# First six attention steps: bonus sums on TensorE, value copies on ScalarE, two weight pieces and the constants through ScalarE's queue

## The chip, the cores and the metric

One NeuronCore of one Trainium2 chip runs the whole program. The metric is the device time of one execution in microseconds (us). The engines are TensorE (PE in the rows, with its weight loads as PEld), VectorE (DVE), ScalarE (ACT), GpSimd (POOL) and SyncE (SP), which here only issues DMAs.

## The reference, cut to what matters

Three layers follow each other: a linear attention with a decaying state (4 batches, 8 heads, 768 tokens, 48 channels a head), a feed-forward layer with softplus (3072 tokens, 384 to 2048 to 384), and a layer of 8 experts with a greedy capacity-limited assignment.

```
for t in range(S):                                   # attention
    cur = einsum('bhd,bhe->bhde', u[None] * k_t, v_t)
    y[:, :, t] = einsum('bhd,bhde->bhe', r_t, state + cur)
    state = w[None, :, :, None] * state + einsum('bhd,bhe->bhde', k_t, v_t)
h = x @ w_in                                         # feed-forward
x = (maximum(h, 0) + log1p(exp(-abs(h)))) @ w_out
logits = x @ w_gate                                  # then the choice of an expert for each token,
out[mask] = maximum(x[mask] @ w1[e], 0) @ w2[e]      # and its two matmuls
```

The term `cur` is the bonus: for each token and head the sum over d of r·u·k, times the value row. Feed-forward weights arrive as 64-bit floats and are rebuilt to 32 bits with integer operations.

## The kernel before, in words

**Attention.** 24 steps of 128 rows each: step n takes 64 tokens of a pair of batches. `load_step` issues eight 96 KB DMAs for a step, all on SP's queue: k, r and v by token (tiles `kn`, `rn`, `vn`, line 367, two each) and v again in another layout (tile `X`, line 373, two). `attention(n)` then multiplies k and r by tables of powers (`ks`, `rs`, line 340), transposes both on PE (lines 466 and 470), copies them out of PSUM (`kT`, `ar`), multiplies (line 491), masks on DVE (`ar`, line 499), updates the state (lines 520, 525 and 527, copied into the next `X`) and forms the output (line 553). The bonus runs on DVE: `rk` = r·k, `rk`·`ut`, a reduction to `sd` (line 543), and `sv` = v·`sd`; line 558 adds `sv` to the output and makes `xf`. `xf` is transposed (line 566) into `xt`, the input of the feed-forward layer.

**Feed-forward.** 8 blocks of 384 tokens, three attention steps each. Block 0 runs in 32-bit floats, while the weights are being rebuilt: `from_double` loads a 384 KB piece into one of four buffers (tile `third`; line 607 for the first matrix, `w_in`, 16 pieces; line 624 for the second, `w_out`, 16 pieces) and rebuilds it with three DVE instructions (lines 599, 601 and 603). `ffn1(0, f)` (line 673) needs the transposed outputs of steps 0, 1 and 2 and piece f. Later blocks use split 16-bit weights (line 678). Blocks overlap: while block b runs its first matmul, block b-1 or b-2 runs its second, and the attention steps of a later block are woven in.

**What sets the order.** Every piece of work is an item with an engine (or a choice of two), an assumed duration, dependencies and a due time. `lay_out` plays the schedule through with the assumed durations, picks at each point the ready item with the earliest due time, and writes each engine's instruction stream in that order; on the chip every engine runs its stream in order and waits on semaphores. The due times come from `due_att`, `due_ffn1`, `due_ffn2` and a table of leads (`T0`, `ATT0`, `LOADL`, `AHEAD`, `HALFL`, `BITL`, `OUTLATE` and so on). `keep_warm` puts matmuls on a zero tile (`still`, line 143) into the gaps of the planned PE stream; their results are not used. All DMAs share eight completion semaphores in turn, so the ninth DMA waits at its issue for the first to land.

Of the kernel before, what the change touches and what calls it, by code (L numbers as in the profile page):

```python
# [21 lines left out]
def tile_kernel(ctx, tc, r, k, v, w, u, w_in, w_out, w_gate, w1, w2, out):  # L22
# [10 lines left out]
    HP = H // 2  # L33
# [114 lines left out]
    def lay_out(todo, rank, clock, warm=False):  # L148
# [91 lines left out]

    ACT.add_instruction(mybir.InstLoadActFuncSet(
        name=nc.get_next_instruction_name(), engine=mybir.EngineType.Activation, ins=[], outs=[],
        act_func_set_id=[a.name for a in SETS].index("natural_log_exp_and_others")))

# [5 lines left out]

    T0 = 15500.0
    LEN0 = 43500.0
# [20 lines left out]

    AHEAD = 7500.0

    TURNED, TURN = 6, 1500.0
    HALFL = 4000.0
    HALFL2 = -4000.0
    NLAT = 6
    LATL = 400.0  # L280
    OUTLATE = 5000.0
    RAWL = 17600.0
    BITL = 14000.0
    SPLITL = -3900.0
    WOUTL = 6100.0
    ATT0 = 2600.0
    LOADL = 1600.0

# [18 lines left out]
    XF = several(work, 2, [128, H * D], FT, "xf")  # L307
    XHL = several(work, 2, [128, 2 * DM], HF, "xhl")
    XT2 = several(ffn1p, 2, [128, 2 * KC, BT], HF, "xt")
# [50 lines left out]
    def load_step(n):  # L360
        GROUP[0] = "att"
        b0, s0 = step_tok(n)
        i = n % 2
        due = due_att(n) - LOADL
        for key, src, store in (("kn", k, KN), ("rn", r, RN), ("vn", v, VN)):
            for b in range(2):
                op("sp", 650.0, lambda b=b, src=src, store=store: SP.dma_start(
                    store[i][b * 64:(b + 1) * 64], src[b0 + b, :, s0:s0 + C, :].rearrange("h s d -> s h d")),
                    w=[(key, i, b)], due=due, size=546.0)
        for q in range(2):  # L370
            src = bass.AP(tensor=v.tensor, offset=v.offset + ((b0 * H + q) * S + s0) * D,
                          ap=[[D, C], [2 * S * D, 2 * HP], [1, D]])
            op("sp", 650.0, lambda q=q, src=src: SP.dma_start(
                X[n % 3][(1 - q) * 64:(2 - q) * 64, q].rearrange("p b a d -> p (b a) d"), src),
                w=[("xv", n % 3, q)], due=due + 3.0, size=546.0)

# [12 lines left out]
    DVE.memset(wt, 1.0)  # L389
    op("sp", 1300.0, lambda: [SP.dma_start(wt[q * 64:q * 64 + D], w.rearrange("(p q) d -> q d p", q=2)[q])  # L390
                              for q in range(2)], w=["wt"], due=-1e9, size=168.0)
    op("sp", 450.0, lambda: SP.dma_start(
        ut, bass.AP(tensor=u.tensor, offset=u.offset, ap=[[0, 128], [1, H * D]])), w=["ut"], due=-500.0, size=546.0)
    op("sp", 450.0, lambda: SP.dma_start(gate, w_gate.rearrange("(k p) e -> p k e", p=128)),
# [17 lines left out]
    def powers():  # L412
# [5 lines left out]
        for i in range(6):  # L418
# [3 lines left out]
            DVE.tensor_mul(pw[:, 1, :, C - 2 * m:C - m], pw[:, 1, :, C - m:C], f)  # L422

    op("dve", 3200.0, powers, r=["wt"], w=["pw", ("ar", 1, 0)], due=-1e8)

# [18 lines left out]
    def attention(n):  # L444
# [62 lines left out]
        if n % PC < PC - 1:  # L507
# [27 lines left out]
            for q in range(2):  # L535
                rows = slice(q * 64, (q + 1) * 64)
                op({"act": 413.0, "dve": 470.0}, 0.0, lambda eng, rows=rows, q=q: copied(eng, X[y][rows, q], wx[rows].rearrange("p a b d -> p b a d")),
                   r=[("wx", 0), ("wx", 1)], w=[("st", y, q)], due=due + 3)


        product(rk, RN[i], KN[i], rnk + knk, ["rk"], due + 3)
        product(rk, rk, ut.rearrange("p (h d) -> p h d", h=H), ["ut"], ["rk"], due + 3)
        op("dve", 470.0, lambda: DVE.tensor_reduce(sd, rk, axis=AX.X, op=OP.add), r=["rk"], w=[("sd", i)], due=due + 3)
        product(sv, VN[i], sd[:, :, None].to_broadcast([128, H, D]), vnk + [("sd", i)], [("sv", i)], due + 3)

# [35 lines left out]
        else:  # L581
            xh, xl = XHL[i][:, :DM], XHL[i][:, DM:]
            op(FROM_SBUF, 0.0, lambda eng: scaled(eng, xh, xf, 64.0), r=[("xf", i)], w=[("xhl", i, 0)], due=due + 5)
            op("dve", 470.0, lambda: DVE.scalar_tensor_tensor(xl, xf, 64.0, xh, op0=OP.mult, op1=OP.subtract),
# [8 lines left out]
    def from_double(src, t, key, due):  # L593
        c = WN[0]
        WN[0] += 1
        raw = RAW[c % 4]
        op("sp", 450.0, lambda: src(raw), w=[("raw", c % 4)], due=due - RAWL, size=1092.0)
        hi, lo = [raw[..., i] if len(t.shape) == 2 else raw[..., i].rearrange("p (k f) -> p k f", k=KC) for i in (1, 0)]
# [7 lines left out]
    def prep_win(j):  # L606
        from_double(lambda raw: SP.dma_start(
            raw.rearrange("p (k f) t -> p k (f t)", k=KC),
            w_in.rearrange("(k p) f -> p k f", p=128)[:, :, 256 * j:256 * (j + 1)]),
            WF32[j].bitcast(I32), ("wi", j + 1), due_ffn1(0, j))  # L610
# [10 lines left out]
    def prep_wout(f):  # L621
        due = due_ffn2(0, 0, f) - WOUTL
        t = WU32[f]
        from_double(lambda raw: SP.dma_start(
            raw.rearrange("p m t -> p (m t)"), w_out.rearrange("(c p) m -> c p m", p=128)[f]),
# [14 lines left out]
        op(FROM_PSUM, 0.0, lambda eng: copied(eng, wT, b1.view(KC, 128)), w=[wt], due=due, bank=b1)  # L640
        op("pe", 330.0, mm, r=[wt, "gate"], due=due, bank=b2)
        op("act", 58.0, lambda: ACT.copy(t[:, DM:], b2.view(E)), w=[("wg", f + 1)], due=due, bank=b2)
# [741 lines left out]
    for p in range(E):  # L1384
# [7 lines left out]
        experts(p)  # L1392
    total = lay_out(items, lambda it: (it.prio, it.n), {}, True)
    s_ps.close()
# [24 lines left out]
```

## Time and profile before

| | |
|---|---|
| median of 3 runs | 778.96 us (777.51 to 786.61) |
| the profiled execution, its own time | 775.64 us |
| its span, first to last instruction | 773.9 us |
| mean granted TensorE clock | 0.996 |
| busy: PE / weight loads / DVE / ACT / POOL | 749.8 / 493.0 / 624.9 / 404.1 / 81.2 us |

The span is what the trace covers; the execution's own time is 1.7 us longer. PE's busy time contains the zero matmuls of line 143 and is modelled at its ends, so its idle time is read together with the chain of waits.

### The profile page before, as it was taken

Reading aid. Unit: us, or ns where it says so; the run is one execution under the profiler, and the core shown is the slowest. Engines: PE = TensorE matmul, PEld = TensorE weight load, DVE = VectorE, ACT = ScalarE, POOL = GpSimd, SP = SyncE. Lnnn points to the kernel's source line nnn. Section 1 sums busy time; section 2 is a strip of 40 time slices with the busy share of each in tenths; the row PEclk is TensorE's granted clock in tenths of the full one; section 3 lists DMA queues with packets and bytes.
Section 4 is the critical chain, followed back from the end, with each engine's and each line's share of the span. In section 5 each row is a group of like instructions: output and inputs, shape, how many; then the busy total and the mean of one; then the engine's idle time right before and its main releaser. Section 6 shows DMA issues by size and latency. Waiting matters only on the chain.

```text
span 773.9 us, 18327 instructions
## 1 busy us (share of the span) xinstructions
PE 749.8 (97%) x7202; PEld 493.0 (64%) x7202; DVE 624.9 (81%) x1711; ACT 404.1 (52%) x808; POOL 81.2 (10%) x109
## 2 busy tenths in 40 slices
PE   7999999999999999999999999999999999998996
PEld 6865677666566666667676666666666665655663
DVE  7898998999998787788999977887789879877420
ACT  2165533799766666567889911211145424436731
POOL 1000000000000000000001000000232131317731
PEclk9999999999999999999999999999999999999999
DMA  7887764412343233333110003441385664837700
GB/s 137 172 183 191 211 171 77 83 22 62 69 91 66 56 68 62 62 67 71 36 22 11 2 12 94 118 121 50 97 208 165 174 175 143 211 108 191 216 31 30
DMA packets 170901, 80.04 MB, mean 103 GB/s; under 512 B 136512, under 2 KB 166464, under 8 KB 170816
## 3 DMA queue, kind: packets, MB, share of 16 engines
q1 hardware_dynamic: 167744, 69.44, 38.3%
q0 software_dynamic: 3072, 9.44, 4.0%
q8 instruction: 56, 0.92, 0.5%
q14 instruction: 29, 0.24, 0.1%
HBM read 61.55 MB, written 9.63 MB: 92 GB/s over the span
## 4 chain that ended last, share of the span: by engine, by line
PE 67%; DVE 18%; issue 4%; ACT 4%; DMA 4%; SPq 1%; POOL 1%; POOLq 0%; ACTq 0%; DVEq 0%
PE bank L678 14%; PE bank L1292 7%; PE bank L788 7%; PE bank L789 6%; PE bank L790 6%; PE bank L785 3%; PE bank L1310 3%; PE bank L1312 3%; PE bank L1311 3%; PE bank L553 2%; PE bank L673 2%; DVE ar L499 2%; DVE gf L691 2%; PE bank L1036 2%; DMA mraw<-moe_w 1%
## 5 line engine op out<-in xcount | busy, mean ns | idle before, releaser
L678 PEld LDWEIGHTS <-wi 128*128 128x128 f16 x1008 | 97.3, 98 | 65.2 <-issue 2.0
L678 PE MATMUL bank<-xt,wi 128*128 128x384 f16 x672 | 127.6, 326 | 0.0
L684 ACT ACTIVATE ta<-bank 128x384 f32<-128x384 f32 x128 | 61.5, 482 | 43.3 <-PE bank L678 30.2
L789 PE MATMUL bank<-wo,g 128*128 128x384 f16 (+1 forms) x240 | 78.4, 327 | 0.9 <-DVE wo L649 0.7
L788 PE MATMUL bank<-wo,g 128*128 128x384 f16 (+1 forms) x240 | 78.5, 327 | 0.0
L790 PE MATMUL bank<-wo,g 128*128 128x384 f16 (+1 forms) x240 | 78.5, 327 | 0.0
L691 DVE SCALAR_TENSOR_TENSOR gf<-bank,ta 128x384 f32<-128x384 f32 x112 | 61.8, 553 | 17.2 <-ACT ta L686 16.0
L678 PE MATMUL bank<-xs,wi 128*128 128x384 f16 x336 | 72.9, 326 | 0.0
L1292 PE MATMUL bank<-g,w1h 128*128 128x384 f16 x384 | 72.9, 326 | 0.0
L685 ACT ACTIVATE ta<-ta 128x384 f32<-128x384 f32 x128 | 66.5, 522 | 2.9
L686 ACT ACTIVATE ta<-ta 128x384 f32<-128x384 f32 x128 | 66.2, 519 | 2.5
L1312 PE MATMUL bank<-w2h,g 128*128 128x384 f16 x192 | 62.6, 326 | 0.0
L1310 PE MATMUL bank<-w2h,g 128*128 128x384 f16 x192 | 62.6, 326 | 0.0
L1311 PE MATMUL bank<-w2l,g 128*128 128x384 f16 x192 | 62.5, 326 | 0.0
L1296 ACT ACTIVATE g<-bank 128x384 f16<-128x384 f32 x64 | 30.7, 489 | 40.4 <-PE bank L1292 24.7
L1292 PEld LDWEIGHTS <-w1h 128*128 128x128 f16 x384 | 35.8, 98 | 22.6 <-issue 0.4
L1299 DVE SCALAR_TENSOR_TENSOR g<-bank,g 128x384 f16<-128x384 f32 x64 | 34.1, 548 | 19.4 <-ACT g L1296 19.3
L698 DVE SCALAR_TENSOR_TENSOR g<-gf,g 128x384 f16<-128x384 f32 x80 | 44.0, 553 | 3.1 <-ACT g L345 1.8
L499 DVE TENSOR_TENSOR ar<-bank,mask 64x256 f32<-64x256 f32 x96 | 40.5, 422 | 4.6 <-PE bank L491 2.3
L345 ACT ACTIVATE x2o<-bank 128x384 f16<-128x384 f32 x19 | 9.3, 490 | 65.3 <-PE bank L790 39.2
L1205 POOL DMA_INDIRECT third<-x2d,idx x24 | 25.8, 1074 | 155.7 <-DVE db L1009 130.0
L1292 PE MATMUL bank<-g,w1l 128*128 128x384 f16 x192 | 41.7, 326 | 0.0
(227 smaller groups left out, 1533.3 us busy)
## 6 DMA issues: line engine op xcount, KB each, us to landing
mraw<-moe_w SPq DMA_DIRECT2D x64, 384.0 KB, 4.0
third<-moe_w_in SPq DMA_DIRECT2D x16, 384.0 KB, 5.0
third<-moe_w_out SPq DMA_DIRECT2D x16, 384.0 KB, 3.5
kn<-k SPq DMA_DIRECT2D x48, 96.0 KB, 3.1
rn<-r SPq DMA_DIRECT2D x48, 96.0 KB, 3.1
vn<-v SPq DMA_DIRECT2D x48, 96.0 KB, 3.0
X<-v SPq DMA_DIRECT2D x48, 96.0 KB, 3.1
x2d<-x2o SPq DMA_DIRECT2D x48, 96.0 KB, 2.2
```

The lines of the kernel that those rows point to most:

```text
L678: PE.matmul(ph, WF[:, f, a, kk, :], x[:, kk, :], start=(i == 0), stop=(i == 3 * KC - 1))
L684: op("act", 371.0, lambda: ACT.activation(ta, bank.view(BT), AF.Abs), w=[("ta", c)], due=due, bank=bank)
L685: op("act", 413.0, lambda: ACT.activation(ta, ta, AF.Exp, scale=-1.0), w=[("ta", c)], due=due)
L686: op("act", 413.0, lambda: ACT.activation(ta, ta, AF.Ln, bias=1.0), w=[("ta", c)], due=due)
L691: op("dve", 470.0, lambda: DVE.scalar_tensor_tensor(gf, bank.view(BT), 0.0, ta, op0=OP.max, op1=OP.add), r=[("ta", c)], w=[("gf", c)], due ...
L788: PE.matmul(p, gh[:, f, ts], WU[:, f, 0, :no], start=(f == 0), stop=False)
L789: PE.matmul(p, gh[:, f, ts], WU[:, f, 1, :no], start=False, stop=False)
L790: PE.matmul(p, gl[:, f, ts], WU[:, f, 0, :no], start=False, stop=(f == FC - 1))
L1292: PE.matmul(ph, a[:, kk, fs], XH[p][:, x0 + kk, :], start=(i == 0), stop=(i == 3 * KC - 1))
L1310: PE.matmul(po, h1h[:, f, js], w2h[:, fz, :], start=(f == 0), stop=False)
L1311: PE.matmul(po, h1h[:, f, js], w2l[:, fz, :], start=False, stop=False)
L1312: PE.matmul(po, h1l[:, f, js], w2h[:, fz, :], start=False, stop=(f == FB - 1))
```

## The change

- In steps 0 to 5 the bonus no longer multiplies r by k by token. `rkT` = the transposed r (still in PSUM, bank b2) times `kT`, one DVE instruction of 128x512; then four PE matmuls of 128x128 by 128x2 against a small matrix `uw` (u times w, one column for each of the two heads of a pair) put the sums into a bank, and `sv` reads them from PSUM. `rkT` lives in the storage of `xhl`, which steps from 6 on use.
- In the same steps the second load of v is gone; four copies of 64x192 out of `vn` fill `X` instead, each planned on ScalarE or VectorE, whichever is free.
- The DMAs of w (`wt`), a new small load of u (`uq`) and the first two pieces of `w_in` are issued by ScalarE. The activation table's load becomes an item behind them. The broadcast load of u (`ut`) comes later, before step 3.
- Due times and assumed sizes are new, and the planner's clocks of SP and DVE start at 1000 and 900 ns.

```diff
-    ACT.add_instruction(mybir.InstLoadActFuncSet(
+    op("act", 1290.0, lambda: ACT.add_instruction(mybir.InstLoadActFuncSet(
...
-    T0 = 15500.0
+    T0 = 16250.0
...
-    AHEAD = 7500.0
+    AHEAD = 10500.0
...
-    HALFL = 4000.0
-    HALFL2 = -4000.0
+    COPIED = 6
+    AHEADW = 2
+    HALFL = 9000.0
+    HALFL2 = -1500.0
...
-    OUTLATE = 5000.0
+    OUTLATE = 8750.0
...
-    BITL = 14000.0
+    BITL = 16000.0
...
-    ATT0 = 2600.0
-    LOADL = 1600.0
+    ATT0 = 850.0
+    LOADL = 2400.0
...
+        if n < COPIED:
+            for q in range(2):
+                for b in range(2):
+                    op({"act": 260.0, "dve": 180.0}, 0.0, lambda eng, q=q, b=b: copied(
+                        eng, X[n % 3][(1 - q) * 64:(2 - q) * 64, q, b],
+                        VN[i][b * 64:(b + 1) * 64].rearrange("p (a q) d -> p a q d", q=2)[:, :, q, :]),
+                        r=[("vn", i, b)], w=[("xv", n % 3, q)], due=due_att(n) + 2.5)
+            return
...
-    op("sp", 1300.0, lambda: [SP.dma_start(wt[q * 64:q * 64 + D], w.rearrange("(p q) d -> q d p", q=2)[q])
-                              for q in range(2)], w=["wt"], due=-1e9, size=168.0)
+
+    op("act", 900.0, lambda: [ACT.dma_start(wt[q * 64:q * 64 + D], w.rearrange("(p q) d -> q d p", q=2)[q])
+                              for q in range(2)], w=["wt"], due=-3e9, size=168.0)
+    op("act", 900.0, lambda: [ACT.dma_start(uq[q * 64:q * 64 + D], u.rearrange("(p q) d -> q d p", q=2)[q])
+                              for q in range(2)], w=["uq"], due=-2e9, size=168.0)
...
+    def factors():
+        DVE.memset(uw, 0.0)
+        for q in range(2):
+            DVE.tensor_mul(uw[q * 64:q * 64 + D, :, q], uq[q * 64:q * 64 + D], wt[q * 64:q * 64 + D])
...
+        if n < TURNED:
+            op("dve", 602.0, lambda: DVE.tensor_tensor(rkT, b2.view(HP, 128), kT, op=OP.mult), r=[("kT", i)], w=["rkT"],
+               due=due + 3, bank=b2)
+
+            def sums():
+                for pr in range(HP):
+                    PE.matmul(b7.view(H)[:, 2 * pr:2 * pr + 2], rkT[:, pr, :], uw[:, pr, :], start=True, stop=True)
+
+            b7 = Bank("att")
+            op("pe", 900.0, sums, r=["rkT", "uw"], w=[("sd", i)], due=due + 3, bank=b7)
+            op("dve", 470.0, lambda: DVE.tensor_tensor(sv, VN[i], b7.view(H)[:, :, None].to_broadcast([128, H, D]), op=OP.mult),
+               r=vnk, w=[("sv", i)], due=due + 3, bank=b7)
+        else:
+            bonus()
...
-        op("sp", 450.0, lambda: src(raw), w=[("raw", c % 4)], due=due - RAWL, size=1092.0)
+        eng = "act" if c < AHEADW else "sp"
+        op(eng, 450.0, lambda: src(ACT if eng == "act" else SP, raw), w=[("raw", c % 4)], due=due - RAWL, size=1900.0)
...
-    total = lay_out(items, lambda it: (it.prio, it.n), {}, True)
+    total = lay_out(items, lambda it: (it.prio, it.n), {"sp": 1000.0, "dve": 900.0}, True)
```

How the streams move shows best at the program's start. SP's stream before, from its first DMA on (a row is line, tile, source, shape, repeats):

```order
L390 DMA wt<-w 48x4x1 x2
L607 DMA third<-moe_w_in 128x3x256
L367 DMA kn_93<-k 64x8x48 x2
L367 DMA rn_91<-r 64x8x48 x2
L367 DMA vn_95<-v 64x8x48 x2
L373 DMA X_97<-v 64x8x48 x2
L392 DMA ut<-u 128x384
L607 DMA third<-moe_w_in 128x3x256
L367 DMA kn_94<-k 64x8x48 x2
L367 DMA rn_92<-r 64x8x48 x2
L367 DMA vn_96<-v 64x8x48 x2
```

The same place in SP's stream after the change:

```order
L370 DMA kn_92<-k 64x8x48 x2
L370 DMA rn_90<-r 64x8x48 x2
L370 DMA vn_94<-v 64x8x48 x2
L370 DMA kn_93<-k 64x8x48 x2
L370 DMA rn_91<-r 64x8x48 x2
L370 DMA vn_95<-v 64x8x48 x2
L370 DMA kn_92<-k 64x8x48 x2
L370 DMA rn_90<-r 64x8x48 x2
L649 DMA third<-moe_w_in 128x3x256 x3
L406 DMA ut<-u 128x384
```

Step 1's loads now stand behind six other transfers, where they stood behind thirteen; the weights follow behind step 2's k and r. ScalarE's stream, which began with the table load and went straight to the copies of the power tables, now begins:

```order
L402 DMA wt<-w 48x4x1 x2
L404 DMA uq<-u 48x4x1 x2
L241 ACT_TABLE_LOAD
L649 DMA third<-moe_w_in 128x3x256 x2
L354 COPY pwn_145<-bank_80 128x512
L354 COPY pwn_144<-bank_81 128x512
L354 COPY kT_108<-bank_82 128x512
L354 COPY ar_110<-bank_83 64x8x64
L354 COPY X_96<-vn_94 64x192 x3
```

The four small loads and the two pieces of weights stand ahead of the first copy. VectorE's stream before, from the end of the power tables on:

```order
L599 TENSOR_SCALAR wi<-third 128x384
L428 COPY kT_110<-ar_112 128x512
L601 SCALAR_TENSOR_TENSOR wi<-third,wi 128x384
L340 TENSOR_TENSOR rk_104<-rn_91,kn_93 128x384
L428 COPY kT_110<-ar_112 128x512
L603 SCALAR_TENSOR_TENSOR wi<-third,wi 128x384
L340 TENSOR_TENSOR ks_102<-kn_93,pwn_147 128x8x48
L347 TENSOR_SCALAR wi<-wi 128x384
L340 TENSOR_TENSOR rs_100<-rn_91,pwn_146 128x8x48
L340 TENSOR_TENSOR rk_104<-rk_104,ut 128x384
```

And after the change:

```order
L444 MEMSET uw 128x8
L446 TENSOR_TENSOR uw<-uq,wt 48x4 x2
L453 COPY kT_109<-ar_111 128x512 x2
L641 TENSOR_SCALAR wi<-third 128x384
L343 TENSOR_TENSOR ks_101<-kn_92,pwn_145 128x8x48
L643 SCALAR_TENSOR_TENSOR wi<-third,wi 128x384
L343 TENSOR_TENSOR rs_99<-rn_90,pwn_144 128x8x48
L645 SCALAR_TENSOR_TENSOR wi<-third,wi 128x384
L641 TENSOR_SCALAR wi<-third 128x384
L356 COPY X_96<-vn_94 64x192
L356 COPY ar_110<-bank_83 64x8x64
L573 TENSOR_TENSOR xhl<-bank_83,kT_108 128x512
```

The `rk` products are gone, the first weight conversion now stands in front of `ks` of step 0, and the `rkT` product (shown as `xhl`, whose storage it uses) stands behind the copy of `ar`. Up to the addition of step 2 (line 558 before, 599 after) VectorE's stream holds 12 conversion instructions where it held 8, two copies of `ar` out of a bank where it held three, one copy of the state into `X` where it held three, and three copies of `vn` into `X`. PE's stream holds 210 zero matmuls ahead of the first feed-forward matmul where it held 258, and 60 behind it where it held 76. In later blocks the same matmuls are ordered otherwise: the output of one step (line 553) now mostly stands next to the state update of the next.

## Rows read from the trace of the kernel before

**Rows 1.** Windows: start:end, length, busy (count) by engine, clock, DMA share, GB/s.

```profile
0.00:10.00 10.00, 7.21 (x86) 6.73 (x87) 8.37 (x35) 2.34 (x3) 2.53 (x12) 1.00 0.62 126
10.00:20.00 10.00, 7.12 (x138) 6.18 (x141) 6.51 (x14) 2.38 (x5) 0.00 (x0) 0.87 0.84 161
...
30.00:40.00 10.00, 9.76 (x182) 8.24 (x180) 9.52 (x23) 2.51 (x5) 0.00 (x0) 1.00 0.72 135
40.00:60.00 20.00, 20.00 (x160) 12.63 (x159) 17.33 (x42) 13.53 (x27) 0.00 (x0) 1.00 0.92 200
60.00:80.00 20.00, 17.84 (x157) 11.03 (x156) 19.64 (x47) 9.40 (x20) 0.00 (x0) 1.00 0.64 166
...
150.00:200.00 50.00, 49.31 (x451) 30.73 (x449) 48.88 (x116) 46.69 (x108) 0.82 (x2) 1.00 0.22 44
```

**Rows 2.** Chain of work that ended last, 0 to 110 us: start, us, what.

```profile
9.75 6.74 DMA kn<-k
...
37.27 0.57 DVE xf L558
...
39.00 4.14 PE bank L673 x12
...
55.73 3.95 DMA third<-moe_w_in
...
78.26 2.20 PE bank L673 x6
```

**Rows 3.** Timeline of SP's queue: start, us of issue, line, transfer, count.

```profile
1.01 0.89 SPq L390 DMA_DIRECT2D wt<-w  x2
1.94 0.45 SPq L607 DMA_DIRECT2D third<-moe_w_in  x1
...
6.60 1.31 SPq L373 DMA_DIRECT2D X<-v  x2
7.96 0.62 SPq L392 DMA_DIRECT2D ut<-u  x1
```

**Rows 4.** Timeline of DVE, steps 0 and 1; in brackets the wait before.

```profile
9.17 0.55 DVE L340 TENSOR_TENSOR ks<-kn,pwn 128x384 f32<-128x384 f32 x1
...
12.56 0.56 DVE L340 TENSOR_TENSOR rk<-rk,ut 128x384 f32<-128x384 f32 x1 [1.85 <-DMA ut<-u]
...
16.59 0.56 DVE L340 TENSOR_TENSOR ks<-kn,pwn 128x384 f32<-128x384 f32 x1 [1.26 <-DMA kn<-k]
```

**Rows 5.** Groups by line and shape, 0 to 62 us: busy us, mean ns.

```profile
L601 DVE SCALAR_TENSOR_TENSOR wi<-third,wi 128x384 int32<-128x384 int32 x11 | 6.0, 550 | 0.0
L599 DVE TENSOR_SCALAR wi<-third 128x384 int32<-128x384 int32 x11 | 3.9, 354 | 2.4 <-DMA third<-moe_w_in 2.4
L353 DVE COPY ar<-bank 64x512 f32<-64x512 f32 x4 | 2.8, 691 | 0.9 <-ACT ar L351 0.9
L543 DVE TENSOR_REDUCE sd<-rk 128x8 f32<-128x384 f32 x4 | 2.2, 550 | 0.1
L340 DVE TENSOR_TENSOR rk<-rk,ut 128x384 f32<-128x384 f32 x4 | 2.2, 550 | 1.8 <-DMA ut<-u 1.8
L351 ACT COPY X<-wx 64x384 f32<-64x384 f32 x4 | 2.0, 512 | 6.3 <-DVE wx L340 5.0 <-DVE wx L525 1.3
L353 DVE COPY X<-wx 64x384 f32<-64x384 f32 x4 | 1.4, 356 | 0.1
L241 ACT ACT_TABLE_LOAD x1 | 1.3, 1283 | 0.8 <-PEq L1406 0.8
```

**Rows 6.** Timeline of PE: start, us, line, operation, count, wait before.

```profile
24.38 2.02 PE L143 MATMUL bank<-still 128*128 128x128 bf16 x33
...
62.46 0.66 PE L466 MATMUL bank<-identf,ks 128*128 128x128 f32 x4 [1.56 <-DVE ks L340]
...
78.26 2.20 PE L673 MATMUL bank<-xt,wi 128*128 128x384 f32 x6 [0.34 <-DVE wi L603]
...
81.36 1.50 PE L637 MATMUL bank<-gate,third 128*128 128x8 f32 x12
```

## What I predict, before the changed kernel has run

> **What bounds the kernel now.** I read the windows first [rows 1]. From 40 us on PE is busy almost without a break: 20.00 of 20 us, 17.84 of 20, 49.31 of 50. Before 40 us it is not the bound: 7.21 and 7.12 us of the first two tens, and much of that is zero matmuls. There VectorE is the one that fills up, from 6.51 us in the second ten to 9.52 in the fourth. So the program is a front of 39 us without feed-forward work, then about 735 us of PE work, and whatever shortens the front shortens the whole, as long as PE keeps its work afterwards.
>
> The chain of waits says what the front hangs on [rows 2]. Step 1's k was issued by SP until 9.75 us and took 6.74 us to land; then the chain runs through VectorE to the addition of step 2 at 37.27, and the first feed-forward matmul starts at 39.00. At 55.73 the chain is on a DMA of a weight piece for another 3.95 us, and from 78.26 on it stays on PE within the stretch shown. The timelines show what these waits cost: VectorE stood 1.85 us for the broadcast of u and 1.26 us for step 1's k [rows 4]; PE stood 1.56 us at 62.46 and 0.34 us at 78.26, both for VectorE, which had stood 2.4 us for a weight piece [rows 5, 6].
>
> **The change in the front.** VectorE's work up to step 2's addition, counted by its stream:
> - Gone are two products and a reduction in each of three steps: 9 x 0.550 = 4.95 us [rows 5]. `sv` stays.
> - New are three `rkT` products of 128x512 out of PSUM. No row shows this operation. The nearest is the copy out of a bank of 512 columns, 0.691 us; a product of 384 columns, 0.550, is the lower bound. I take 0.691: +2.07.
> - One bank copy and two state copies fewer: -0.691 - 2 x 0.356 = -1.40 us. Three copies of 64x192 more: between nothing and the 0.356 of twice the elements, I take 0.2: +0.6. Three tiny operations for `uw`, each below 0.354: +0.4 in all.
> - Four more weight conversions of 0.550 come ahead of that point: +2.2.
>
> Sum: -4.95 + 2.07 - 1.40 + 0.6 + 0.4 + 2.2 = **-1.1 us**. The bonus alone is lighter by 2.9, but the planner fills most of it with conversions which otherwise come later.
>
> The two DMA waits, **-3.1 us**. The broadcast of u is not read in these steps, so 1.85 goes. Step 1's k was the 14th transfer of SP's queue and is the 7th now. The first 10 us moved 1.26 MB and the next ten 0.161 MB per us [rows 1]; ahead of and with step 1's k there are now eight loads of 96 KB and two pieces of 384 KB, 1.57 MB, which by that rate have landed at 10 + 0.31/0.161 = 11.9 us instead of 16.49. VectorE reads it after step 0's work, at 16.59 before [rows 4], so the 1.26 goes with 4 us to spare.
>
> A new wait, **+0.6 us**. The conversion of piece 0 now stands ahead of step 0's `ks` on VectorE, and everything of steps 0 to 2 is queued behind it. ScalarE issues this piece behind four small loads and the table load. No row shows a DMA issued by ScalarE; SP's rows are the nearest, 0.89 us for a pair and 0.45 for a piece [rows 3], and the table load is 1.28 [rows 5]: 1.0 + 2 x 0.89 + 1.28 + 0.45 = 4.5 us. Landing lies between the 3.95 us that the chain shows for a piece and the 6.74 for a load in a crowd [rows 2], so at 8.5 to 11.3 us, where step 0's `ks` ran at 9.17 [rows 4]. The delay is 0 to 2.2 us; piece 0 stands among few transfers, so I take 0.6, from the lower half.
>
> Front: -1.1 - 3.1 + 0.6 = **-3.6 us**, feed-forward from about 35.4 us. The ends: 0.5 us gained, if other waits take the place of the two that go; 5.1, if VectorE also loses its remaining idle time of the second ten (3.49 in all) and the fourth (0.48).
>
> What is hidden there. ScalarE's issuing, 2.7 us for six DMAs at 0.45: it was busy 2.34 of the first ten us. The 24 copies of values, 18 of them on ScalarE at 0.512 at most [rows 5]: it is busy 2.38 of the second ten and 13.53 of 20 from 40 us on. Without that cover, a copy that waits for `vn` would hold the next step's `kT` copy and so PE. SP's vn2, now behind three pieces, `ut` and two stores, must also wait for step 0's `sv`; it is first needed for step 2's state, ten us later. The sums of steps 0 to 2 on PE lie where it has 2.88 of 10 us idle.
>
> **The change after the front.**
> - The sums of steps 3 to 5 are PE work where PE is the bound. The nearest row has 32-bit weights of 128x128 and 8 columns: 6 matmuls (12 records) in 1.50 us [rows 6], so four cost 1.0 us. The four transposes, 0.66 us, are the lower bound. I take 3 x 1.0 = **+3.0 us** (2.0 at the least).
> - PE's two waits between 40 and 80 us, **-1.9 us**. VectorE is relieved of the same 2.9 us in steps 3 to 5 and of the 2.2 us of conversions done early, and the DMA engines of twelve loads, 1.18 MB, which at 200 GB/s is 5.9 us of transfers against a start only 3.6 us earlier. At worst nothing of this comes.
> - 16 zero matmuls fewer behind the first feed-forward matmul; 33 of them took 2.02 us [rows 6]: **-1.0 us**, at worst 0.
> - The new due times of blocks 2 to 7 order the same matmuls otherwise. I cost them at nothing, because VectorE and ScalarE run ahead of PE there. The cover is thin in one place: from 150 to 200 us VectorE is busy 48.88 and ScalarE 46.69 of 50 [rows 1]. There 0.7 us of PE's idle time could be won, or, if a planned order misses, a stall like that of 60 to 80 us, 2.2 us, come in.
>
> **Sum.** -3.6 + 3.0 - 1.9 - 1.0 = **-3.5 us** against the profiled execution, 775.64 to 772.1. The median of the three runs lies 3.3 us above that execution; I move it by the same amount: 778.96 - 3.5 = **775.5 us**, 0.4% faster.
>
> **Rivals.**
> The forecast is that issue and work on VectorE set the front. **The transfers set it anyway**: the engines' share is 0.84 in the second ten and 0.92 from 40 to 60 us [rows 1], so loads issued earlier may only land in the same order at the same rate, and the waits move to other loads. Then the front gains 0.5, PE's waits stay, and the sum is -0.5 + 3.0 - 1.0 = +1.5: 780.5 us. Against it: SP issues back to back, 0.89, 0.45, 1.31, 0.62 us [rows 3], and fewer bytes stand ahead of step 1. The Trainium skill (DMA: Bandwidth & Descriptors, Issuing engines are not separate DMA queues) says that DMAs of all issuing engines run on the same 16 engines and that a second issuer saves only the issue time; by that, ScalarE's queue brings no bandwidth, and this rival is what it would come to. The trace agrees as far as it goes: the crowded load took 6.74 us.
>
> **The other side: ScalarE's queue is late.** If piece 0 lands late, VectorE's stream stands at the first conversion, `ks` of step 0 waits behind it, and each us delays all. Without this wait my sum is -4.1, so the kernel gets slower from a landing at about 13.3 us on (9.2 + 4.1). Landing as late as step 1's k did, at 16.49, the wait is 7.3 us: -4.1 + 7.3 = +3.2, 782.2 us. For it: the piece goes out behind five other issues and shares the eight semaphores. Against it: 11.3 us is the worst that the rows give.
>
> **More than forecast**: front -5.1, sums at 2.0, waits of 60 to 80 us all gone (2.16), zero matmuls -1.0: -6.3, 772.7 us. For it: VectorE idles 3.49 us in the second ten. **A miss in a later block** adds 2.2 to the forecast: 777.7.
>
> **How the numbers follow.** Forecast 0.5 (its own range 772 to 779), transfers 0.2, ScalarE's queue 0.12, more than forecast 0.13, a miss later 0.05. To the outer cases I add some 4 us below, and nothing above the late-queue case, whose price is already an extreme: 769 to 782 leaves out about 2 in 10. The measurement of this kernel can tell some 2% from no change, 15.6 us; no case reaches that. Faster by more 0.03, within 0.95, slower 0.02, for mechanisms that I do not see.
>
> **What the changed profile would show.** Right: the first feed-forward matmul at 34 to 37 us; no DVE wait for a load of k or u in step 1; the sums at about 1 us a step; PE busy above 19 of 20 us from 60 to 80. Wrong: step 0's `ks` later than 11 us with a wait for a weight piece (the late queue); the first matmul still at 38 us with waits for other loads (transfers); new PE waits past 100 us (a miss later); a lower granted clock in the front, where fewer zero matmuls run, that lasts beyond the first feed-forward matmul.

## The result and the profile after

The changed kernel takes **772.91 us** (median of 20 executions, 770.77 to 779.39), the kernel before beside it 780.16 (20 executions, where the forecast's 778.96 was the median of three). The ratio is 0.9916, 95% interval 0.9895 to 0.9936: 0.84% faster, about 6.5 us, where 3.5 were forecast. The profiled execution takes 773.06 us, 2.6 less than the profiled one of before. The profiled execution of before (775.64 us) was as quick as the quickest of its 20 and 4.5 us under their median, while that of the changed kernel lies at its median.

The windows of the changed kernel, columns and stretches as in [rows 1]:

```profile
0.00:10.00 10.00, 6.56 (x77) 6.20 (x77) 7.08 (x35) 1.87 (x2) 2.53 (x12) 1.00 0.77 150
10.00:20.00 10.00, 9.52 (x204) 8.45 (x202) 9.24 (x23) 5.50 (x13) 0.00 (x0) 1.00 0.83 177
...
40.00:60.00 20.00, 20.00 (x215) 13.44 (x215) 19.12 (x44) 14.59 (x33) 0.00 (x0) 1.00 0.69 166
60.00:80.00 20.00, 19.86 (x241) 13.72 (x241) 19.75 (x46) 13.55 (x28) 0.00 (x0) 1.00 0.64 158
150.00:200.00 50.00, 50.00 (x458) 31.39 (x457) 47.98 (x113) 40.80 (x93) 0.83 (x2) 1.00 0.36 58
```

VectorE's second ten is full, 9.24 us where it was 6.51; PE's 60 to 80 us are full, 19.86 where it was 17.84. The clock in the second ten is 1.00 where it was 0.87.

The timeline of VectorE in the changed kernel answers to [rows 4] (step 0's `ks`, step 1's `ks`); the bracket is the wait before:

```profile
4.15 0.17 DVE L427 COPY sq<-wt 128x4 f32<-128x4 f32 x1 [0.81 <-DMA wt<-w]
...
8.88 0.43 DVE L453 COPY kT<-ar 128x512 f32<-128x512 f32 x1 [0.75 <-PE bank L459]
9.22 0.35 DVE L641 TENSOR_SCALAR wi<-third 128x384 int32<-128x384 int32 x1
9.50 0.56 DVE L343 TENSOR_TENSOR ks<-kn,pwn 128x384 f32<-128x384 f32 x1
...
12.00 0.25 DVE L356 COPY X<-vn 64x192 f32<-64x192 f32 x1
...
13.32 0.69 DVE L573 TENSOR_TENSOR xhl<-bank,kT 128x512 f32<-128x512 f32 x1
...
17.83 0.56 DVE L343 TENSOR_TENSOR ks<-kn,pwn 128x384 f32<-128x384 f32 x1
```

Piece 0's conversion (9.22) waits for nothing, and step 1's `ks` for no load. The waits that are left are for `w` and for TensorE's transposes.

The timelines of ScalarE's and of SP's queue in the changed kernel answer to [rows 3], the latter at 46 us to the piece of [rows 2] at 55.73:

```profile
1.01 0.93 ACTq L402 DMA_DIRECT2D wt<-w  x2
1.97 1.00 ACTq L404 DMA_DIRECT2D uq<-u  x2
2.99 1.28 ACT L241 ACT_TABLE_LOAD   x1 [2.99 <-DVE identf L418]
3.89 1.17 ACTq L649 DMA_DIRECT2D third<-moe_w_in  x2
```

```profile
46.74 1.21 SPq L649 DMA_DIRECT2D third<-moe_w_in  x1
```

And PE's timeline at the start of feed-forward work answers to [rows 6]:

```profile
35.12 2.20 PE L715 MATMUL bank<-xt,wi 128*128 128x384 f32 x6
...
45.50 1.05 PE L578 MATMUL bank<-uw,xhl 128*128 128x2 f32 x8
```

Between the two profiled executions the landmarks move as follows (starts of the matmuls named, us):

| | before | after | moved |
|---|---|---|---|
| first feed-forward matmul | 39.0 | 35.1 | -3.9 |
| first one of block 1 | 142.4 | 140.0 | -2.4 |
| last of the second product, all blocks | 553.3 | 548.6 | -4.7 |
| first of the experts | 557.8 | 554.7 | -3.1 |
| span | 773.9 | 771.0 | -2.9 |

So 3.9 us were won in front, another 0.8 net up to 549 us, and 1.8 were given back from there on, 1.6 of them ahead of the experts' first matmul.

### The profile page after: what moved, and what is told of

The parts are those of the page before. It is cut to its first block, busy times and chain, and to the rows that moved or that the text cites. A ratio compares the mean times of both kernels' runs of the same rounds, so it can differ in the third digit from the quotient of the medians.

```text
span 771.0 us, 18329 instructions
## 1 busy us (share of the span) xinstructions
PE 750.0 (97%) x7186; PEld 493.0 (64%) x7186; DVE 623.7 (81%) x1720; ACT 403.6 (52%) x814; POOL 80.4 (10%) x109
## 3 DMA queue, kind: packets, MB, share of 16 engines
q1 hardware_dynamic: 160192, 67.47, 37.4%
## 4 chain that ended last, share of the span: by engine, by line
PE 68%; DVE 19%; issue 4%; DMA 3%; ACT 3%; POOL 1%; POOLq 0%; SPq 0%; ACTq 0%; DVEq 0%
PE bank L720 18%; PE bank L830 7%; PE bank L1334 7%; PE bank L831 7%; PE bank L832 7%; PE bank L827 4%; PE bank L1352 3%; PE bank L1354 3%; PE bank L1353 3%; DMA mraw<-moe_w 2%; DVE ar L524 2%; PE bank L1078 2%; PE bank L594 2%; PE bank L679 1%; PE bank L516 1%
## 5 line engine op out<-in xcount | busy, mean ns | idle before, releaser
L348 ACT ACTIVATE x2o<-bank 128x384 f16<-128x384 f32 x21 | 10.2, 485 | 63.7 <-PE bank L832 38.3
```

## The experiments

**All parts and their combinations.** The change has three parts that can be had apart: the values copied instead of loaded, the bonus on TensorE, and the new due times. The first three runs take one part away each. The new assumed sizes and the planner's start clocks stay in every version made from the changed kernel; no run takes them out.

`x_by_dma`, the changed kernel with the values loaded again:

```diff
-    COPIED = 6
+    COPIED = 0
```

> The changed kernel with the twelve second loads of v as DMAs again, no copies. If the front hangs on VectorE's work, the first feed-forward matmul moves by no more than 1 us (0.6 us less VectorE work, step 1's loads behind two more transfers). If transfers set it, 98 KB x 6 more by step 2 at 0.161 MB per us make it 3 to 4 us later, 38 to 39 us, and the kernel loses most of its gain.

`no_bonus`, the changed kernel with the bonus on VectorE in all steps (and `ut` early again):

```diff
+    BONUS = 0
...
-        ut, bass.AP(tensor=u.tensor, offset=u.offset, ap=[[0, 128], [1, H * D]])), w=["ut"], due=due_att(3), size=1200.0)
+        ut, bass.AP(tensor=u.tensor, offset=u.offset, ap=[[0, 128], [1, H * D]])), w=["ut"], due=-500.0, size=1200.0)
...
-        if n < TURNED:
+        if n < BONUS:
```

> The changed kernel with the bonus back on VectorE in all steps (u broadcast early again), all else as changed. If VectorE's work sets the front, it grows by 2.9 us (three steps of 4.95/3 - 0.69) and by the 1.85 us wait if u's broadcast is late, so the first feed-forward matmul comes at 38 to 40 us instead of 35.1; the three 1.0 us sums leave PE after it. Time: about 1 us above the changed kernel, between it and before. If transfers set the front, the first feed-forward matmul stays at 35 to 36 us and the kernel is up to 3 us faster than the changed one.

`old_due`, the changed kernel with the due times of before:

```diff
-    T0 = 16250.0
+    T0 = 15500.0
...
-    AHEAD = 10500.0
+    AHEAD = 7500.0
...
-    HALFL = 9000.0
-    HALFL2 = -1500.0
+    HALFL = 4000.0
+    HALFL2 = -4000.0
...
-    OUTLATE = 8750.0
+    OUTLATE = 5000.0
...
-    BITL = 16000.0
+    BITL = 14000.0
...
-    ATT0 = 850.0
-    LOADL = 2400.0
+    ATT0 = 2600.0
+    LOADL = 1600.0
```

> The changed kernel with the old table of due times (T0, AHEAD, HALFL, HALFL2, OUTLATE, BITL, ATT0, LOADL). My forecast put the new table of the later blocks at nothing: then from the first feed-forward matmul to the end it takes as long as the changed kernel, within 1.5 us. If the table carries the gain between 80 and 446 us (there the changed kernel gained another 1.7 us over before), it is 2 to 4 us slower than the changed kernel.

Each loses the gain, as far as can be measured: all three intervals in the table below contain 1, and none reaches down to 0.9936, the upper end of the changed kernel's. The expectations held in part. `x_by_dma`'s first feed-forward matmul moved by only 0.5 us, as expected if VectorE's work sets the front, and yet its time is the longest. `no_bonus` was to lie about 1 us above the changed kernel with feed-forward work from 38 to 40 us; it lies 4.5 above, with 37.2. `old_due` was to be as fast behind the first feed-forward matmul if the table is worth nothing, and is not.

Two more have one part alone: `new_due` is the kernel before with the eight new numbers (the diff above, backwards), `copies_alone` is `no_bonus` with the old numbers, so it has ScalarE's queue too. The bonus alone was not run.

> The kernel before with only the new table of due times: bonus on VectorE, values, constants and all weight pieces through SP's queue as before. Measured so far against before: all of the change 0.992 (about -6.5 us), all but the table 1.000. Table theory (the table by itself carries the gain): about 773 to 775 us, -4 to -6. Joint theory (the table only pays with the loads that go away in the front, because it asks for attention work and weights earlier than twelve more loads leave room for): no gain or a loss, 778 to 783, with VectorE and PE waiting for loads before 100 us. Clock theory (the table saves through fewer short stands of PE, each followed by some us at half clock): the mean granted clock of its runs is nearer to the 0.996 of the changed kernel than to the 0.992 of before, whatever the front does.

> Of the change only the copies of the values in place of twelve loads and the three loads through ScalarE's queue; bonus on VectorE in all steps, due times as before. Medians so far: nothing changed 779.1, table alone 779.1, copies and bonus 777.1, copies and table 777.5, bonus and table without the copies 780.9, all three 772.9. Theory that SP's queue sets 40 to 80 us of before (the eleventh piece of w_in is issued at 55.7 us there and at 46.7 in the changed kernel, and VectorE waits 2.4 to 4.3 us for it in before, however early the front ends): the piece is issued before 50 us, no wait of VectorE for it, PE's wait of 1.6 to 3.4 us at 62 us gone, and the time 776 to 778; VectorE, with the bonus still on it, then sets the pace between 40 and 100 us. If the three parts simply added up, the copies' share would be 779.1 less the 6.2 of all three, less what the others bring (0 and about 2): some 775. If the transfers don't matter: 779.

| kernel | copies | bonus on PE | new due | median us | ratio to before, 95% | 11th piece of `w_in` issued | first feed-forward matmul | PE busy of 40 to 500 us | zero matmuls |
|---|---|---|---|---|---|---|---|---|---|
| before | - | - | - | 780.16 | 1 | 55.73 | 39.0 | 455.49 | 11.5 |
| new_due | - | - | x | 779.11 | 0.9986 to 1.0038 | 55.09 | 37.7 | 454.90 | 14.6 |
| copies_alone | x | - | - | 778.22 | 0.9967 to 1.0025 | 49.38 | 36.7 | 455.65 | 14.1 |
| x_by_dma | - | x | x | 780.92 | 0.9992 to 1.0058 | 57.58 | 34.6 | 456.54 | 14.0 |
| no_bonus | x | - | x | 777.45 | 0.9955 to 1.0022 | 49.95 | 37.2 | 456.85 | 12.8 |
| old_due | x | x | - | 777.09 | 0.9973 to 1.0032 | 48.81 | 35.3 | 455.78 | 10.2 |
| after | x | x | x | 772.91 | 0.9895 to 0.9936 | 46.74 | 35.1 | 458.58 | 9.5 |

Each ratio is to executions of the kernel before taken beside that version; over all the runs their medians lie between 776.77 and 780.16, so the ratios compare better than the medians. The last column is PE's time on zero matmuls, in us, from the first feed-forward matmul to the last of the second product.

None of the five versions with one or two of the parts can be told from the kernel before; all three together bring 0.84%. The columns say where they differ. Without the copies the eleventh piece of `w_in` goes out at 55 to 58 us, with them at 46 to 50. The two versions without the bonus on TensorE that have the copies, and `new_due`, begin feed-forward work at 36.7 to 37.7 us, those with it near 35. And PE stands for more than 3 us of the 460 in every one of them but the whole change, 1.4 there.

Standing is not all of PE's idle time. The planner fills gaps that it foresees with zero matmuls, which count as busy. The windows of line 143 alone, from the first feed-forward matmul to the last of the second product, for before, the changed kernel and `x_by_dma` (start:end, length, PE and its weight loads with counts, clock, DMA share, GB/s):

```profile
39.00:553.30 514.30, 11.50 (x60) 5.62 (x60) 1.00 0.36 81
```

```profile
35.10:548.60 513.50, 9.48 (x45) 4.30 (x44) 1.00 0.35 78
```

```profile
34.60:555.80 521.20, 14.00 (x119) 8.87 (x119) 1.00 0.37 81
```

This places the losses against the changed kernel, whose stretch is 513.5 us long. `x_by_dma` needs 521.2: 4.5 us more of zero matmuls, 1.4 more of standing, and a clock of 0.93 and 0.90 from 390 to 410 us, worth some 1.7. `no_bonus` needs 515.5, behind a front 2.1 us longer: 3.3 more of zero matmuls and 1.1 of standing, less 2.4 of other work. `old_due` needs 519.0: 2.1 more of standing, 0.7 of zero matmuls, and a clock of 0.91 over the 40 us from 40 to 80, worth some 3. So what one part frees is lost at another place when a second part is missing, and partly as gaps that the plan already holds. Why the plan has them is not shown.

The expectation for `copies_alone` held in each row it named, piece before 50 us, no wait of VectorE for it, PE busy 19.51 of 20 us from 60 to 80. The time was unchanged all the same, so the wait for the piece does not carry the gain by itself. `no_bonus` says the same: there PE is busy 39.75 of the 40 us from 40 to 80.

**ScalarE's queue.** `sp_queue` issues the two weight pieces, `w` and `u` from SP again.

```diff
-    AHEADW = 2
+    AHEADW = 0
...
-    op("act", 900.0, lambda: [ACT.dma_start(wt[q * 64:q * 64 + D], w.rearrange("(p q) d -> q d p", q=2)[q])
+    op("sp", 900.0, lambda: [SP.dma_start(wt[q * 64:q * 64 + D], w.rearrange("(p q) d -> q d p", q=2)[q])
...
-    op("act", 900.0, lambda: [ACT.dma_start(uq[q * 64:q * 64 + D], u.rearrange("(p q) d -> q d p", q=2)[q])
+    op("sp", 900.0, lambda: [SP.dma_start(uq[q * 64:q * 64 + D], u.rearrange("(p q) d -> q d p", q=2)[q])
```

> The changed kernel with the constants and the two weight pieces issued by SP. SP's issue grows by 2 x 0.95 + 2 x 0.5 = 2.9 us ahead of or among steps 0 and 1. If only issue time counts, step 1's k lands up to 3 us later, at about 15 us, still ahead of its use at 17.8: first feed-forward matmul within 1 us of 35.1. If ScalarE's queue brings bandwidth or earlier landing, the first matmul is 3 us later or more.

773.72 us, ratio 0.9941 (0.9911 to 0.997), first feed-forward matmul at 35.3, within the expected 1 us: what the queue is worth lies within the error. It does move one wait. In `sp_queue` the powers wait for nothing, and step 0's `ks` starts at 8.90; in the changed kernel they wait 0.81 us for `w`, and `ks` starts at 9.50. VectorE's timeline of `sp_queue`:

```profile
3.44 0.17 DVE L427 COPY sq<-wt 128x4 f32<-128x4 f32 x1
```

**Which due times.** Three runs put a group of them back in the changed kernel: `due_att` the leads of attention (AHEAD, OUTLATE), `due_weights` those of the weights (HALFL, HALFL2, BITL), `due_start` those of the start (T0, ATT0, LOADL).

> The changed kernel with the leads of attention alone as before (AHEAD 10500 to 7500: steps of blocks 2 to 7 are due 3 us later; OUTLATE 8750 to 5000: their outputs' conversions 3.75 us earlier behind them). If the table's gain lies in the leads of attention, about 776 to 777 us and a mean clock near 0.994 as with the whole old table; if it lies in the weights' leads or at the start, 773, as the changed kernel.

> The changed kernel with the leads of the weights' halves alone as before (HALFL 9000 to 4000, HALFL2 -1500 to -4000, BITL 16000 to 14000: the 16-bit halves of the weights are converted 2 to 5 us later). If the table's gain lies here, 776 to 777 us, with VectorE's and ScalarE's conversions late at the start of block 1 (140 us) and of the second product (175 us); if not, 773.

> The changed kernel with the due times of the start alone as before (T0 16250 to 15500, ATT0 850 to 2600 a step, LOADL 2400 to 1600: steps 0 to 5 due later, their loads with less lead). Theory that the table works through the first 100 us: feed-forward work starts at 35.3 us all the same, but PE waits between 40 and 100 us come back with some us at half clock behind each (as the whole old table had 0.46 us of wait at 62.70 and then 3.39 us for six matmuls that take 2.20 at full clock): 776 to 777 us. Otherwise 773.

| | median us | ratio to before, 95% | PE busy of 40 to 500 us | of 150 to 200 us |
|---|---|---|---|---|
| due_att | 774.29 | 0.9910 to 0.9965 | 456.73 | 49.77 |
| due_weights | 775.77 | 0.9934 to 0.9998 | 455.13 | 48.04 |
| due_start | 775.40 | 0.9930 to 1.0001 | 456.28 | 48.76 |
| old_due, all back | 777.09 | 0.9973 to 1.0032 | 455.78 | 50.00 |

No single group carries the gain. Weights and start cost about 2.5 to 3 us each when put back, attention 1.4, and these three differences lie within their intervals. Where the weights' leads are old, PE stands at 150 to 200 us, the place that I had named as thin. `due_start` did not do what was expected of it: feed-forward work begins at 36.8 us instead of 35.3, with the bonus on TensorE, and from 40 to 80 us PE stands only 0.3 us.

**The clock in front, and the kernel before once more.** `front_warm` is the kernel before with 30 more zero matmuls ahead of step 1's first transposes; `before_again` is the kernel before, unchanged, profiled a second time.

```diff
+            self.warm = 0
...
-            k = int((it.start - last - 100.0) / step)
+            k = int((it.start - last - 100.0) / step) + it.warm
...
-        op("pe", 428.0, tk, r=[("ks", i), "ident"], w=[("kT", i)], due=due + 2, bank=b1)
+        op("pe", 428.0, tk, r=[("ks", i), "ident"], w=[("kT", i)], due=due + 2, bank=b1).warm = 30 if n == 1 else 0
```

> The kernel before with 30 more zero matmuls on TensorE ahead of step 1's first transposes (nothing else changed). In before PE was busy 0.71 of 2 us from 16 to 18 us and had half the clock from 18 to 20. Clock theory (a part of the front's gain, and of the 3 us by which the profiled execution of before lies under its median, is granted clock in the front): the clock stays at 1.00 from 14 to 24 us, feed-forward work starts 1 to 2 us earlier, at 37 to 38 us, and the median falls to 776 to 778. Theory that the front hangs on VectorE and loads alone: the start stays at 39.0 and the median at 779; the added matmuls, about 1.8 us, lie in idle time.

> The kernel before, unchanged, profiled once more. Its profiled execution took 775.64 us while the median of its runs is 779, and the runs' times fall with their mean granted clock (0.984 at 788 us, 0.999 at 773.5). Clock theory of the spread: an execution nearer the median shows the same waits, and more stretches at half clock behind short stands of PE; each 1 us at half clock costs 0.5. Other theory: loads land later in some executions, and PE or VectorE wait for them.

`front_warm`: 775.51 us, ratio 0.9977 (0.9952 to 1.0001), which can't be told from before, clock 1.00 from 10 to 30 us, first feed-forward matmul at 36.8. `before_again`: one execution, 778.68 us, span 776.9, near the median of before. It also kept the clock in front, without the extra matmuls, and its feed-forward work began at 37.4 us. But both lose that again. First VectorE's, then PE's timeline of `before_again`, then its windows:

```profile
60.03 0.36 DVE L599 TENSOR_SCALAR wi<-third 128x384 int32<-128x384 int32 x1 [4.26 <-DMA third<-moe_w_in]
```

```profile
62.78 1.11 PE L466 MATMUL bank<-identf,ks 128*128 128x128 f32 x4 [3.45 <-DVE ks L340]
```

```profile
60.00:62.00 2.00, 0.00 (x0) 0.00 (x0) 1.97 (x5) 0.12 (x1) 0.00 (x0) 1.00 0.87 303
62.00:64.00 2.00, 1.22 (x6) 1.23 (x7) 2.00 (x6) 0.45 (x2) 0.00 (x0) 0.64 0.68 210
64.00:66.00 2.00, 2.00 (x38) 1.61 (x37) 1.47 (x3) 1.70 (x4) 0.00 (x0) 0.51 0.74 215
```

The piece of the eleventh issue goes out at 56.23 us, no earlier than in the first execution (55.73), because SP issues it behind the loads of later steps. VectorE, which comes 1.6 us earlier, waits 4.26 us for it instead of 2.4 [rows 5], PE 3.45 instead of 1.56 [rows 6], and behind this stand PE's clock is 0.64 and 0.51 in two windows of 2 us, the second about the lower of its two levels, 1.2 of 2.4 GHz. In `front_warm` it is 4.1 us of waiting, and block 1 starts at 142.3, as in before.

The long wait alone does not make a long execution, though. The profiled one of `front_warm` took only 772.37 us. Its second product ends like that of before (553.1 and 553.3 us); 3.1 us of its lead lie behind that, in the experts, where these kernels do not differ. Over all fourteen profiles the time from the last matmul of the second product to the end runs from 217.5 to 224.1 us.

**Half of the sums.** `sums3` keeps the bonus on TensorE in steps 0 to 2 alone.

```diff
+    BONUS = 3
...
-        if n < TURNED:
+        if n < BONUS:
```

> The changed kernel with the bonus on TensorE in steps 0 to 2 alone; steps 3 to 5 as before on VectorE. It takes three groups of sums (1.05 us each by the trace, 3.15 together) off PE where PE has no idle time, and gives VectorE back 2.9 us in a stretch where it is busy 39 of 40 us. If PE's work is what counts there (the term of the forecast): 771 to 772 us, 1 to 2 below the changed kernel. If VectorE sets the pace from 40 to 80 us: PE waits appear there, 2.9 us of them less what VectorE has idle, and the time is 773 to 776.

772.17 us (771.42 to 775.69, 8 executions), and a span of 769.9 in its profile; PE is busy 39.64 of the 40 us from 40 to 80. The number is that of the first theory, but the trace is not. The windows of line 143 for `sums3`, to be read beside those above:

```profile
34.90:549.60 514.70, 12.79 (x92) 7.49 (x91) 1.00 0.34 78
```

The three sums, 3.15 us, are gone from PE, and 3.3 us more of zero matmuls stand in their place; from the first feed-forward matmul to the last of the second product it takes 514.7 us, 1.2 more than in the changed kernel. So PE's work is not shown to be what counts there, and what the sums cost in time stays open. The kernel before beside it was at 776.77, and the ratio 0.9948 (0.9914 to 0.9982) overlaps that of the changed kernel: no better version is shown.

## Why the prediction was right, and where it was not

All four signs of being right came: feed-forward work from 35.1 us, no wait of VectorE for k or u in step 1, sums of 1.05 us, and PE busy 19.86 of 20 us from 60 to 80. What failed is the step from the profile to the median, and luck had a part in the sum.

**The front: right in its sum, partly by luck.** Forecast -3.6, measured -3.9 against the first profile of before; against `before_again`, whose feed-forward work begins at 37.4, it is -2.3. The windows from the start to the end of step 2's addition, first of before, then of `before_again`, then of the changed kernel (the third busy time is VectorE's):

```profile
0.00:37.84 37.84, 31.62 (x574) 28.20 (x574) 30.65 (x85) 8.34 (x14) 2.53 (x12) 0.95 0.78 158
```

```profile
0.00:36.27 36.27, 30.26 (x574) 27.02 (x574) 30.54 (x85) 8.34 (x14) 2.53 (x12) 1.00 0.81 159
```

```profile
0.00:33.96 33.96, 29.53 (x550) 26.93 (x550) 29.45 (x85) 12.83 (x26) 2.53 (x12) 1.00 0.80 174
```

VectorE's work fell by 30.65 - 29.45 = 1.20 us; forecast 1.1. Each operation that no row had shown came near its bound or value: `rkT` 0.69 (0.691 taken), the copy of 64x192 0.25 (0.2 taken), `uw` 0.40 together (0.4). Only the four conversions were 2.0 and not 2.2, since one of them is the shorter kind. VectorE's idle time fell by 7.19 - 4.51 = 2.68 us; forecast 3.1 - 0.6 = 2.5. But this second agreement is partly luck. Against `before_again`, whose clock did not fall in front, the idle time fell only from 5.73 to 4.51, 1.2 us, though it has the same two waits (1.67 and 1.31 us). The windows of PE behind step 1's wait, first of before, then of `before_again`:

```profile
16.00:18.00 2.00, 0.71 (x4) 0.70 (x5) 1.35 (x3) 0.00 (x0) 0.00 (x0) 0.86 0.46 80
18.00:20.00 2.00, 2.00 (x34) 1.77 (x35) 1.91 (x5) 0.59 (x1) 0.00 (x0) 0.50 0.98 222
```

```profile
16.00:18.00 2.00, 0.90 (x12) 0.92 (x13) 1.51 (x4) 0.23 (x1) 0.00 (x0) 1.00 0.56 100
18.00:20.00 2.00, 2.00 (x72) 1.80 (x69) 1.91 (x5) 0.35 (x1) 0.00 (x0) 1.00 0.99 252
```

So some 1.5 us of the first execution's idle time came from PE at half clock: the same 12 zero matmuls take 1.49 us there (from 18.03) and 0.83 in `before_again`. No term of the forecast held that. Of the 3.1 us of waits that went, about half came back as others: 0.81 us for `w`, where it was 0.16, and 0.75 for the first transposes, above.

**The new wait: wrong place, and its size a coincidence.** The +0.6 was booked for weight piece 0. Nothing waits for that piece; the powers wait 0.81 us for `w`, for which they waited 0.16 before and not at all in `sp_queue`. Step 0's `ks` starts at 9.50 instead of 9.17. The rival of the late queue is out.

**The transfers.** The rival that loads only land in the old order at the old rate is out for the whole change: no load is waited for in step 1, and PE's waits went. The Trainium skill (DMA: Bandwidth & Descriptors, Issuing engines are not separate DMA queues) had stood behind it: another issuing engine brings no bandwidth. `sp_queue` agrees, 773.72 with all issues on SP. What the rival missed is that the copies take loads out of SP's list: the eleventh piece goes out 9 us earlier. Where only the front gets shorter and the list stays, as in `front_warm` and `before_again`, the rival describes what happens: the wait moves and grows.

**The sums.** Forecast 3 x 1.0, measured 1.05 us a step as work on PE. That this work costs as much time is not shown (`sums3`).

**PE's waits from 40 to 80 us: right on the pair, not the same in each execution.** Booked -1.9, read from one execution; between the two profiles it is 37.84 to 39.86, -2.0. But in `before_again` PE is busy only 19.33 and 16.05 of these two twenties, 4.6 us of standing, and by the two windows above the clock takes another 0.36 of 1.22 and 0.49 of 2.00 us, 1.4: 6.0 against 0.14 in the changed kernel. The wait is a difference of two times that don't move together: when VectorE arrives, and when SP's list lets the piece out. The step that failed is the last one of the sum, moving the median by the profile's difference: it took for granted that the difference is the same in all executions. The two profiles of before show that it isn't: against the first the span falls by 2.9 us, against the second by 5.9.

**The due times, booked at nothing, and the zero matmuls, -1.0.** From the first feed-forward matmul to the last of the second product it is 514.3 us before and 513.5 after, -0.8, where my terms give +3.0 - 1.9 - 1.0 = +0.1. The windows of all work in this stretch, before and after:

```profile
39.00:553.30 514.30, 509.79 (x5154) 335.18 (x5155) 445.80 (x1176) 299.89 (x634) 6.17 (x14) 1.00 0.36 81
```

```profile
35.10:548.60 513.50, 511.42 (x5164) 336.49 (x5164) 445.96 (x1184) 294.97 (x628) 4.81 (x13) 1.00 0.35 78
```

PE's standing fell from 4.5 to 2.1 us (-2.4, booked -1.9), its zero matmuls from 11.5 to 9.5 (-2.0, booked -1.0), and its other work grew from 498.3 to 501.9 (+3.6, booked +3.0). The zero matmuls were priced by a dense row, 0.06 us each; behind the first feed-forward matmul they show 0.19 us each, since many stand alone.

What the new order of the later blocks is worth by itself no term shows. Without the new table the time is that of before (`old_due`), though the table alone brings nothing (`new_due`). So it isn't an edit with a price of its own. I read it as letting VectorE use the room that the other two make, which is argued and not shown: `old_due` starts feed-forward work at 35.3 us, and by block 1 (146.5 us) the lead is gone. An example from its PE timeline:

```profile
62.70 1.47 PE L594 MATMUL bank<-X,ar 128*64 128x48 f32 x28 [0.46 <-DVE ar L524]
64.11 1.10 PE L545 MATMUL bank<-vn,ks 64*64 64x48 f32 x32
65.14 3.39 PE L715 MATMUL bank<-xt,wi 128*128 128x384 f32 x6
```

After half a microsecond of standing, six matmuls that take 2.20 us in the changed kernel take 3.39.

**Not foreseen: 1.8 us given back at the experts.** PE ends the second product 4.7 us earlier, but the first gather of tokens is only 2.9 us earlier (546.4 after 549.3); in the chain it hangs on the selection, and that on a load of the experts' weights (`mraw`). From the chain of waits of the changed kernel, then from its PE timeline:

```profile
506.58 5.55 DMA mraw<-moe_w
...
546.40 1.12 POOL third L1247
...
549.09 3.02 DMA third<-x2d,idx
```

```profile
550.88 0.23 PE L1377 MATMUL bank<-identh,third 128*128 128x128 f16 x1 [0.67 <-DMA third<-x2d,idx]
552.16 0.23 PE L1377 MATMUL bank<-identh,third 128*128 128x128 f16 x1 [1.05 <-DMA third<-x2d,idx]
```

PE stands 1.7 us for the gathered rows, where it stood 0.3 before. That the change does this is not shown: from the last matmul of the second product to the first of the experts it is 6.1 us in this profile and 5.8 in `before_again`, and 4.4 to 4.6 in the other twelve, `sp_queue`, `due_att` and `sums3` among them. It looks like a matter of the single execution.

**In sum.** Between the profiles: -3.9 - 0.8 + 1.8 = -2.9 in span, against -3.5. The sum was right on the pair that it was made from, with errors that partly cancel: the half clock in front (1.5) and less idle time on PE than booked on one side, the waits that came back in front and the experts (1.8) on the other. Against `before_again`, whose time is near the median of before, the span falls by 5.9 us, close to the 6.5 of the medians: 2.3 in front, 4.8 from there to the last of the second product, less 1.2 lost behind it. That the executions near the median of before all hold such a longer wait is likely from this one and not shown, and `front_warm` warns against it. How much of the rest is clock and how much standing the runs don't settle: the mean granted clock is 0.9934 in 34 executions of before (those beside the runs of the due times) and 0.9959 in the 20 of after, which by 774 us is 1.9 us.

## What to carry to other kernels

Price a wait on a load by when the queue lets the load out, not by how long one profile shows the engine standing: if the front gets shorter and the list doesn't, the wait grows by about as much (here 1.9 us more for a VectorE 1.6 us earlier). Profile the kernel before twice when the wait is what you mean to remove, and see how the profiled execution lies to the median. And where loads, VectorE and the order each are nearly full, test the parts together before dropping one that brings nothing alone: here none of the five versions with one or two of three brought anything that could be measured, and the three 0.84%. Count planned filler as idle time when you compare plans: a busy PE hid 9.5 to 14.6 us of it.

## What the runs showed of the hardware

- The granted clock can fall to its lower level behind a short stand of PE: 0.46 us of waiting at 62 us in `old_due`, then 0.58, 0.50, 0.50 and 0.71 in the four microseconds from 64 to 68. It is not the same in each execution of one program: it fell to 0.50 from 18 to 20 us in one profile of before and stayed at 1.00 in the other, behind 0.71 and 0.90 us of PE's work in the two us ahead. What decides this stays open.
- DMA issues by ScalarE, which no row of before showed: 0.93 and 1.00 us a pair, 0.47 (`old_due`) to 0.58 a piece, beside 0.89 and 0.45 on SP [rows 3].
- The two loads of `w`, issued from 1.0 us on, could be read by 3.44 us when SP issued them ahead of k (`sp_queue`), and by 4.15 when ScalarE issued them while SP issued k from 0.76 us on.
- Four products of 128x128 with 128x2, in 32 bits, take 1.05 us (eight records) at full clock, about what the nearest row with 128x8 gave [rows 6].
